# Attention and mixture of experts on one core: the value product's bank is emptied before the step's second row maximum, row maxima are transposed two steps behind, and the preparation of a pair is spread

## The chip, the cores and the metric

The kernel runs on one core of a Trainium2 chip. The metric is the device time of one execution in microseconds, here the median of three executions. An engine is named as the profile names it: PE (TensorE, matrix products; PEld is its loading of weights), DVE (VectorE), ACT (ScalarE), POOL (GpSimd) and SP, whose queue issues the transfers.

## What is computed

An attention over 8 batches of 8 heads, with queries averaged in twos, and a mixture of experts in which each token takes one of 8 experts:

```
q_pool = q.reshape(B, H, S // 2, 2, D).mean(axis=3)
scores = scale * q_pool @ k^T;  scores -= max(scores)
attn   = exp(scores);  attn /= sum(attn) + 1e-09
x      = attn @ v                      # 4608 tokens of 512
e_idx  = argmax(x @ w_gate)            # one expert for a token
out    = gate_w * sigmoid(x @ w_output_gate)[e_idx] * relu(x @ w1[e]) @ w2[e]
```

B and H are 8, S is 1152 (576 pooled queries), D is 64; an expert's inner width is 1024. Operands are split into a rounded part and a remainder (names ending in h and l), so most products are made of two or three matmuls.

## The kernel before

The 64 heads are taken two at a time: 32 pairs. A pair's work is cut into 18 **steps**, nine for each of its two heads (`body` calls `attention`, then `Moe.run`). A step holds, in the order in which the code records it for PE:

- the scores of 128 keys against 576 queries (L279 and L281, four matmuls into `sps`, a pool of two buffers of two banks each). ACT takes two exponentials of them (L293 and L294, or L285 and L286). In steps 1, 3, 7, 9, 13 and 15 of a pair (table `PLP`) the second exponential goes back into the same banks and DVE subtracts there (L289); in the others POOL subtracts in SBUF (L295) and the banks are free after L294;
- one or two tiles of **row maxima** for the pair after it (L232, two or three matmuls into `mp`, a ring of three banks, and a DVE reduction, L233). Even steps have one, odd steps have two;
- where nine or fifteen tiles are together, the transposing of their maxima (`rows`, L259, in the same ring of three banks), DVE's split of them into two rows (L262, L263) and two small transfers into row 66 and 67 of `qb`, from where the scores of the pair subtract them (L281);
- in even steps a burst of P V (L308 to L310, 15 matmuls for each 128 keys), six steps behind the scores. It sums into one bank, `av`, the only buffer of its pool. The first head's burst begins in step 6 of a pair and the second's in step 16. Ahead of each the bank must have been read by DVE: L317 and L320 make the factor `r`, L323 multiplies and is the last reader;
- pieces of the router's work (`logits`, `router`), in odd steps, which take banks of the same ring (L370, L385, L410).

DVE's small work goes through a list, `fill`. One entry is taken at a step's start and one after each reduction of maxima. The three entries of the bank's emptying (`e0`, `e1`, `e2`) are put at the head of that list when a head's last burst is recorded.

The **preparation** of a pair (loading, rounding on ACT, remainders on POOL, copies through SP's queue) stands in the table `PREP`: a number in thirds of a step, and a name. From pair 5 on (pairs are counted from 0) a third r lies (r - 9) / 3 steps behind the start of the preparation, which is 32 steps ahead of the pair; a pair is 54 thirds long, so r and r + 54 are the same place in consecutive pairs. On ACT are `kh` (two), `qh`, `amax` (two, each with a read of its sum) and `vh` (two).

PE, DVE, ACT and POOL run in the order of the code. SP's queue is ordered by the program's scheduler, which also decides which buffer of a pool a new tile gets; so a change of order can change the banks.

Of the kernel before, what the change touches and what calls it, by code (L numbers as in the profile page):

```python
# [20 lines left out]
L0 = 15.5  # L21
LS = 0.037
RI = 7
PREP = ((0, 'lk'), (12, 'kh', 0), (13, 'kh', 1), (12, 'qsum'), (15, 'kl'), (18, 'dk', 0), (19, 'dk', 1), (21, 'qh'), (26, 'ql'), (26, 'dq', 0), (27, 'dq', 1), (29, 'qd'), (32, 'dl', 0), (33, 'dl', 1),
        (53, 'lv'), (71, 'amax', 0), (74, 'amax', 1), (81, 'gmax'), (82, 'scale', 0), (85, 'scale', 1), (90, 'scale', 2), (93, 'vh', 0), (93, 'vs', 0), (96, 'vh', 1), (97, 'vl', 0), (100, 'vs', 1), (104, 'vl', 1))
BURST = {0: 2, 2: 2, 4: 2, 6: 2, 8: 1, 10: 2, 12: 2, 14: 2, 16: 3}
PLP = (1, 3, 7, 9, 13, 15)
PLPL = (1, 3, 5, 7, 9, 11, 13, 15, 17)
# [3 lines left out]
SKIP = 3  # L32
TS = 256
M_PAD = 1000
TLAG = 1
ALAG = 6
PB = 9
P32 = 6
# [21 lines left out]
def attention(tc, qT, kT, vL, wg, keep, xrows, idscr, cum, pairs, setup, scat, init):  # L60
    nc = tc.nc
    nb = len(pairs) // 4
    with ExitStack() as ctx:
# [36 lines left out]
        def dmaf(o, i):  # L100
            nc.sync.dma_start(out=o.bitcast(F32), in_=i.bitcast(F32))
# [143 lines left out]
        fill = []  # L245
        now = [0]

        def pop(k=1):
            while k and fill:
                fill.pop(0)()  # L250
                k -= 1
# [3 lines left out]
        def rows(force=False):  # L255
            while pend_t and (force or now[0] >= pend_t[0][-1] + TLAG):
                m9, nt, t0, t1, qbf, _ = pend_t.pop(0)
                tp = ps_m.tile([128, 512], F32, name="tp", tag="mp")[0:nt, 0:128]
                nc.tensor.transpose(out=tp, in_=m9[:, 0:nt], identity=ident)  # L259
                mr = sm.tile([5, 2, 128], F32R, name="mr")[0:nt]  # L260
                c0 = 16.0 * SHIFT
                nc.vector.tensor_scalar(out=mr[:, 0], in0=tp, scalar1=c0, scalar2=None, op0=ALU.subtract)  # L262
                nc.vector.scalar_tensor_tensor(out=mr[:, 1], in0=tp, scalar=c0, in1=mr.bitcast(F32)[:, 0], op0=ALU.subtract, op1=ALU.subtract)  # L263
                for j in range(2):
                    dmaf(qbf[66 + j:67 + j, 128 * t0:128 * t1].rearrange("o (t n) -> o t n", n=128), mr[:, j])
# [32 lines left out]
        def av(st, h, xb):  # L298
            vt = st['vt']
            a = ps_a.tile([128, 512], F32, name=f"av{st['n']}", tag="av")  # L300
            av_ = a[:, 0:325].rearrange("p (b x) -> p b x", x=65)
            pop(99)
            for c in range(NC):
                ph, pl = st['ph', h, c], st['pl', h, c]
                for qb in range(5):
                    q0 = 128 * qb if qb < 4 else NQ - 128
                    hi, lo = ph[:, q0:q0 + 128], pl[:, q0:q0 + 128]
                    nc.tensor.matmul(av_[:, qb, 0:65], lhsT=hi, rhs=vt[:, h, c, 0:65], start=c == 0 and qb == 0, stop=False)  # L308
                    nc.tensor.matmul(av_[:, qb, 0:64], lhsT=hi, rhs=vt[:, h, c, 66:130], start=False, stop=False)  # L309
                    nc.tensor.matmul(av_[:, qb, 0:65], lhsT=lo, rhs=vt[:, h, c, 0:65], start=False, stop=c == NC - 1 and qb == 4)  # L310
                if c < NC - 1:
                    yield
            r = sm.tile([128, 5], F32, name="r")
            H = 2 * st['p'][1] + h

            def e0():
                nc.vector.tensor_scalar(out=r, in0=av_[:, :, 64], scalar1=1e-9 * math.exp(SHIFT), scalar2=st['sc'][:, h:h + 1], op0=ALU.add, op1=ALU.mult)  # L317

            def e1():
                nc.vector.reciprocal(out=r, in_=r)  # L320

            def e2():
                nc.vector.tensor_tensor(out=xb[:, :, 64 * H:64 * H + 64], in0=av_[:, :, 0:64], in1=r.unsqueeze(2).broadcast_to([128, 5, 64]), op=ALU.mult)  # L323
                if h == 1:
                    routers.append([logits(st['p'][0], st['p'][1], xb), 0])
            fill[0:0] = [e0, e1, e2]
            pop(IMM)
            yield

# [31 lines left out]
        def logits(b, c, xb):  # L361

            xh = sm.tile([128, NQ], F32R, name="xh", bufs=1)
            xl = sm.tile([128, NQ], F32R, name="xl", bufs=1)
            yield 1
            for c0, c1, grp in ((0, 256, (0, 1)), (256, NQ, (2, 3, 4))):
                tx = psum()
                for i, t in enumerate(grp):
                    x = xb[:, t, 128 * c:128 * c + 128]
                    nc.tensor.transpose(out=tx[:, 128 * i:128 * i + 128], in_=x, identity=ident)  # L370
                d = 0
                for o, w in ((0, c1 - c0),) if c0 == 0 else ((0, 256), (320, 64)):
                    z = slice(c0 + d, c0 + d + w)
                    nc.scalar.copy(out=xh[:, z], in_=tx[:, o:o + w])

                    def sub(o=o, w=w, z=z, tx=tx):
                        nc.vector.tensor_tensor(out=xl[:, z], in0=tx[:, o:o + w], in1=xh.bitcast(F32)[:, z], op=ALU.subtract)
                    fill.insert(0, sub)
                    d += w
                yield 1  # L380
            for c0, c1 in ((0, 256), (256, NQ)):
                pop(99)
                tl = psum()
                for j, x in enumerate((xh, xl)):
                    nc.tensor.matmul(tl[:, 0:c1 - c0], lhsT=wgt[:, c], rhs=x[:, c0:c1], start=j == 0, stop=j == 1)  # L385
                if c == 0:
                    nc.vector.tensor_copy(out=lT[:, c0:c1], in_=tl[0:32, 0:c1 - c0])
                else:
                    nc.vector.tensor_tensor(out=lT[:, c0:c1], in0=tl[0:32, 0:c1 - c0], in1=lT[:, c0:c1], op=ALU.add)
                yield 1  # L390
            if c == 3:
                yield from router(b, xb)
# [111 lines left out]
        NP = len(pairs)  # L504
        pos = dict(m=0)

        def adv(k, g, want):
            while pos[k] < want:
                next(g, None)
                pos[k] += 1  # L510
# [3 lines left out]
        def prep_at(s, ph):  # L514
            u = 3 * (s + SLEAD) + ph
            for n in range(max(u // 54 - 2, 0), min(u // 54 + 2, NP)):
                r = u - 54 * n + min(3 * (LEAD - 15), 2 * n)
                if r == 0:
                    preps[n] = prep(n, PREP)
                if n in preps:  # L520
                    for f in preps[n].pop(r, ()):
                        f()

        E = mybir.EngineType
        with tc.manual_schedule(engines={E.PE, E.DVE, E.Activation, E.Pool}):
            for s in range(-SLEAD, 0):
                for ph in range(3):
                    prep_at(s, ph)
                if s == -RI:
                    for i in (1, 2):  # L530
                        dmaf(QBs[i][64:66], QBs[0][64:66])
                        dmaf(KBs[i][64:68], KBs[0][64:68])
                if s == 1 - SLEAD + INIT:
                    consts()
                    init(0)
                if s >= -int(L0):
                    adv('m', mg, int(1.5 * (s + 1 + L0)))
                    now[0] = s
                    pop(3)
                    rows()  # L540
            for s in range(18 * NP + 14):
                now[0] = s
                live = s < 18 * NP
                if s % 18 == 2 and 0 < s // 18 < 5:
                    init(s // 18)
                while pendv:
                    pendv.pop(0)()
                pop()
                if live:
                    next(sg)  # L550
                prep_at(s, 0)
                mw = min(27 * NP, int(1.5 * (s + 1 + min(LEAD, L0 + LS * s))))
                if pos['m'] < mw:
                    adv('m', mg, pos['m'] + 1)
                prep_at(s, 1)
                adv('m', mg, mw)
                rows()
                j = s - ALAG
                for _ in range(BURST.get(j % 18, 0) if 0 <= j < 18 * NP else 0):
                    next(ag)  # L560
                prep_at(s, 2)
                if not live:
                    pop(3)
                for r in routers:
                    if s % 2 or not live or not r[1]:
                        r[1] = next(r[0], 0)
            pop(99)
            for r in routers:
                for _ in r[0]: pass
# [420 lines left out]
```

## Time and profile before

| | |
|---|---|
| median of three executions | 1624.14 us (1623.79 to 1625.01) |
| the profiled execution | 1624.72 us |
| its span in the trace | 1622.7 us |
| mean granted clock of PE | 0.986 |
| attention, first scores to last | 34 to 1076 us |
| instructions | 42199 |

The time of the profiled execution is its span and some 2 us around it. In the trace a busy PE is not PE at its peak, and the end of a matmul is modelled; so what a wait costs is read from the starts of matmuls. Rows of the timeline give start and duration in us, then engine, line, operation, written tile and read tiles, and in brackets the idle time of the engine before it with what ended it.

### The profile page before, as it was taken

To read this page: it belongs to the slowest core of one execution; us is meant where nothing else is said; L and a number is where in the kernel's file an instruction comes from. 1 tells how busy PE (TensorE), PEld (TensorE's weight loads), DVE (VectorE), ACT (ScalarE), POOL (GpSimd) and SP (SyncE) were. 2 spreads that over 40 slices of the span, in tenths; PEclk is the share of its full clock that TensorE was granted. 3 is DMA by queue.
4 is the path that set the end of the run, shared out by engine and by line. 5 is a ranking of instruction groups with operands and counts; after the bars stand their busy time and mean duration, and the time that the engine had idled before them with its cause. 6 is when DMAs were issued, how large, how long until landed. Compare 5 with 4: busy or idle time off the path is not lost. (4 is left out here: it accounts for less than half of the span.)

```text
span 1622.7 us, 42199 instructions
## 1 busy us (share of the span) xinstructions
PE 1533.1 (94%) x16618; PEld 1411.1 (87%) x16618; DVE 1073.4 (66%) x2222; ACT 1078.5 (66%) x1862; POOL 996.3 (61%) x917
## 2 busy tenths in 40 slices
PE   4999999999999999999999999879999999999997
PEld 4898889888988888888888888868999999999996
DVE  4676776776676676676677767656666566656663
ACT  2887778877878787878777877744445444544541
POOL 4887888788879788879788978634222322232300
PEclk9999999999999999999999999979999999999999
DMA  7765455655566457446645664255454655263600
GB/s 207 217 160 143 133 149 149 156 139 141 152 151 158 124 144 189 129 123 175 158 129 153 161 154 127 83 173 196 168 190 156 213 176 194 94 226 107 208 22 25
DMA packets 88754, 245.48 MB, mean 151 GB/s; under 512 B 13082, under 2 KB 17370, under 8 KB 88546
## 3 DMA queue, kind: packets, MB, share of 16 engines
q1 hardware_dynamic: 78826, 221.07, 48.6%
q0 software_dynamic: 9728, 21.67, 4.2%
q8 instruction: 134, 2.20, 0.6%
q14 instruction: 66, 0.54, 0.1%
HBM read 165.04 MB, written 23.81 MB: 116 GB/s over the span
## 5 line engine op out<-in xcount | busy, mean ns | idle before, releaser
L233 DVE TENSOR_REDUCE pm<-mp 128x1 f32<-128x384 f32 x864 | 457.6, 549 | 263.3 <-PE mp L232 257.7
L295 POOL TENSOR_TENSOR pl<-p,ph 128x576 f16<-128x576 f32 x381 | 490.2, 1287 | 187.8 <-ACT ph L294 155.5
L232 PE MATMUL mp<-ka,qa 128*128 128x384 f32 x960 | 317.7, 347 | 20.2 <-DMA qa<-yq 18.5
L293 ACT ACTIVATE p<-sps 128x576 f32<-128x576 f32 x381 | 251.0, 659 | 116.8 <-PE sps L281 108.3
L308 PEld LDWEIGHTS <-ph 128*128 128x128 f16 x2880 | 262.6, 97 | 74.3 <-DVE xb L323 40.8
L308 PE MATMUL av<-vt,ph 128*128 128x65 f16 x2880 | 297.0, 194 | 23.4 <-DVE xb L323 23.4
L279 PE MATMUL sps<-qa,ka 128*128 128x288 f32 x1152 | 281.6, 326 | 16.7 <-ACT ph L294 10.9
L309 PE MATMUL av<-vt,ph 128*128 128x64 f16 x2880 | 294.7, 195 | 0.0
L310 PE MATMUL av<-vt,pl 128*128 128x65 f16 x2880 | 293.8, 193 | 0.0
L309 PEld LDWEIGHTS <-ph 128*128 128x128 f16 x2880 | 266.2, 97 | 0.4
L310 PEld LDWEIGHTS <-pl 128*128 128x128 f16 x2880 | 266.5, 99 | 0.0
L232 PE MATMUL mp<-kb,qb 66*128 66x384 f32 x768 | 262.5, 342 | 0.6 <-DMA kb<-kp 0.6
L281 PE MATMUL sps<-qb,kb 68*128 68x288 f32 x1152 | 248.5, 298 | 2.8 <-DMA qb<-mr 2.8
L294 ACT ACTIVATE ph<-sps 128x576 f16<-128x576 f32 x381 | 249.3, 654 | 0.0
L279 PEld LDWEIGHTS sps<-qa,ka 128*128 128x128 f32 x1152 | 183.5, 191 | 27.9 <-ACT ph L294 19.2
L764 PE MATMUL hps<-xh,w1h 128*128 128x256 f32 x704 | 200.4, 285 | 0.0
L764 PE MATMUL hps<-xl,w1h 128*128 128x256 f32 x704 | 200.3, 284 | 0.0
L232 PEld LDWEIGHTS mp<-ka,qa 128*128 128x128 f32 x960 | 180.4, 192 | 22.8 <-issue 18.5
L764 PE MATMUL hps<-xh,w1l 128*128 128x256 f32 x704 | 199.6, 284 | 0.0
L767 ACT ACTIVATE hh<-hps 128x512 fp32r<-128x512 f32 x88 | 52.7, 598 | 221.1 <-PE hps L764 221.1
L285 ACT ACTIVATE ph<-sps 128x576 f16<-128x576 f32 x195 | 128.9, 661 | 92.0 <-PE sps L281 89.7
L281 PEld LDWEIGHTS sps<-qb,kb 68*128 68x128 f32 x1152 | 186.7, 191 | 3.2 <-DMA qb<-mr 3.2
(170 smaller groups left out, 3184.6 us busy)
## 6 DMA issues: line engine op xcount, KB each, us to landing
ka<-xk SPq DMA_DIRECT2D x128, 288.0 KB
raw1b<-in_w_dram SPq DMA_DIRECT2D x24, 1024.0 KB
raw2b<-in_w_dram SPq DMA_DIRECT2D x24, 1024.0 KB
raw1a<-in_w_dram SPq DMA_DIRECT2D x22, 1024.0 KB
raw2a<-in_w_dram SPq DMA_DIRECT2D x22, 1024.0 KB
qp<-in_qT_dram SPq DMA_DIRECT2D x32, 576.0 KB
kpf<-in_kT_dram SPq DMA_DIRECT2D x32, 576.0 KB
vp<-in_vL_dram SPq DMA_DIRECT2D x32, 576.0 KB
```

What stands on the lines that cost most here:

```text
L232: nc.tensor.matmul(mp, lhsT=l, rhs=r, start=j == 0, stop=j == len(ops) - 1)
L233: nc.vector.tensor_reduce(out=pm[:, i:i + 1], in_=mp, axis=AX.X, op=ALU.max)
L279: nc.tensor.matmul(sps[:, j, 0:288], lhsT=ka[:, h, ks], rhs=qa[:, o + 288 * j:o + 288 * j + 288], start=True, stop=False)
L281: nc.tensor.matmul(sps[:, j, 0:288], lhsT=kb[:, h, ks], rhs=qb[:, h, 288 * j:288 * j + 288], start=False, stop=True)
L285: nc.scalar.activation(out=ph2, in_=x, func=AF.Exp, scale=1.0 / 16)
L293: nc.scalar.activation(out=p32.rearrange("p (j n) -> p j n", j=2), in_=x, func=AF.Exp, scale=1.0 / 16)
L294: nc.scalar.activation(out=ph2, in_=x, func=AF.Exp, scale=1.0 / 16)
L295: nc.gpsimd.tensor_tensor(out=pl, in0=p32, in1=ph, op=ALU.subtract)
L308: nc.tensor.matmul(av_[:, qb, 0:65], lhsT=hi, rhs=vt[:, h, c, 0:65], start=c == 0 and qb == 0, stop=False)
L309: nc.tensor.matmul(av_[:, qb, 0:64], lhsT=hi, rhs=vt[:, h, c, 66:130], start=False, stop=False)
L310: nc.tensor.matmul(av_[:, qb, 0:65], lhsT=lo, rhs=vt[:, h, c, 0:65], start=False, stop=c == NC - 1 and qb == 4)
L764: nc.tensor.matmul(hp[:, f], lhsT=W1[w][:, c, fs], rhs=d[x][:, c], start=i == 0, stop=i == 11)
```

## The change

It has four parts: the table `PREP` with other distances, `TLAG` 2 in place of 1, two of the three entries of the bank's emptying put into one, and, once the last maxima have been taken, two more entries of the list in each step.

```diff
-PREP = ((0, 'lk'), (12, 'kh', 0), (13, 'kh', 1), (12, 'qsum'), (15, 'kl'), (18, 'dk', 0), (19, 'dk', 1), (21, 'qh'), (26, 'ql'), (26, 'dq', 0), (27, 'dq', 1), (29, 'qd'), (32, 'dl', 0), (33, 'dl', 1),
-        (53, 'lv'), (71, 'amax', 0), (74, 'amax', 1), (81, 'gmax'), (82, 'scale', 0), (85, 'scale', 1), (90, 'scale', 2), (93, 'vh', 0), (93, 'vs', 0), (96, 'vh', 1), (97, 'vl', 0), (100, 'vs', 1), (104, 'vl', 1))
+PREP = ((0, 'lk'), (12, 'kh', 0), (12, 'qsum'), (19, 'kh', 1), (20, 'kl'), (21, 'dk', 0), (22, 'dk', 1), (26, 'qh'), (29, 'ql'), (28, 'dq', 0), (29, 'dq', 1), (32, 'qd'), (33, 'dl', 0), (35, 'dl', 1),
+        (63, 'lv'), (87, 'amax', 0), (93, 'amax', 1), (96, 'gmax'), (98, 'scale', 0), (99, 'scale', 1), (105, 'scale', 2), (106, 'vh', 0), (107, 'vs', 0), (109, 'vl', 0), (112, 'vh', 1), (112, 'vs', 1), (115, 'vl', 1))
...
-TLAG = 1
+TLAG = 2
...
-            def e0():
+            def e01():
                 nc.vector.tensor_scalar(out=r, in0=av_[:, :, 64], scalar1=1e-9 * math.exp(SHIFT), scalar2=st['sc'][:, h:h + 1], op0=ALU.add, op1=ALU.mult)
-
-            def e1():
                 nc.vector.reciprocal(out=r, in_=r)
...
-            fill[0:0] = [e0, e1, e2]
+            fill[0:0] = [e01, e2]
...
                 rows()
+                if pos['m'] == 27 * NP:
+                    pop(2)
```

On DVE, in steps 4 to 6 of pair 11, where the bank of pair 10's second head is emptied (`pm<-mp` are reductions of maxima: the first here is step 4's, the next two are step 5's, the last is step 6's, behind which PE starts the next sum). Before:

```order
L289 TENSOR_TENSOR pl<-sps_7936,ph 128x576
L233 TENSOR_REDUCE pm<-mp_7963 128x1
L317 TENSOR_SCALAR r<-av_7751,sc 128x5
L233 TENSOR_REDUCE pm<-mp_8027 128x1
L320 RECIPROCAL r<-r 128x5
L233 TENSOR_REDUCE pm<-mp_8033 128x1
L323 TENSOR_TENSOR xb<-av_7751,r 128x5x64
L233 TENSOR_REDUCE pm<-mp_8052 128x1
```

And now, at the same place (L318 and L321 are the old L320 and L323):

```order
L289 TENSOR_TENSOR pl<-sps_7934,ph 128x576
L233 TENSOR_REDUCE pm<-mp_7963 128x1
L317 TENSOR_SCALAR r<-av_7745,sc 128x5
L318 RECIPROCAL r<-r 128x5
L233 TENSOR_REDUCE pm<-mp_8028 128x1
L321 TENSOR_TENSOR xb<-av_7745,r 128x5x64
L233 TENSOR_REDUCE pm<-mp_8033 128x1
L233 TENSOR_REDUCE pm<-mp_8050 128x1
```

The bank's last reader has moved from behind both reductions of the step to between them.

On PE, in step 13 of pair 10, between two scores: two tiles of maxima and the router's logits (L385, now L383), which take a bank of the same ring. Before:

```order
L279 MATMUL sps_7658<-qa_125,ka_122 128x288 x2
L281 MATMUL sps_7658<-qb_128,kb_119 128x288 x2
L232 MATMUL mp_7666<-ka_120,qa_123 128x384
L232 MATMUL mp_7666<-kb_117,qb_126 128x384
L232 MATMUL mp_7670<-ka_120,qa_123 128x384
L232 MATMUL mp_7670<-kb_117,qb_126 128x384
L385 MATMUL tp<-xh,wgt 128x320
L385 MATMUL tp<-xl,wgt 128x320
```

And now:

```order
L279 MATMUL sps_7645<-qa_125,ka_122 128x288 x2
L281 MATMUL sps_7645<-qb_128,kb_119 128x288 x2
L232 MATMUL mp_7652<-ka_120,qa_123 128x384
L232 MATMUL mp_7652<-kb_117,qb_126 128x384
L232 MATMUL mp_7656<-ka_120,qa_123 128x384
L232 MATMUL mp_7656<-kb_117,qb_126 128x384
L259 MATMUL tp<-ident,m_7504 5x128
L383 MATMUL tp<-xh,wgt 128x320
L383 MATMUL tp<-xl,wgt 128x320
```

The transposing of the maxima, which stood in step 12 ahead of its burst of P V, has come between the maxima and the logits, so that four tiles of the ring of three banks follow each other. In the built program the logits' bank is the one of the step's first tile of maxima.

On PE, at the scores of step 17 of pair 10, behind the burst of step 16, with the engines whose semaphores an instruction waits for (Activation is ACT). Before:

```order
L310 LDWEIGHTS pl_7522
L310 MATMUL av10_7751<-vt0_138,pl_7522 128x65
L279 MATMUL sps10_7784<-qa1_125,ka1_122 128x288 [waits DVE_49,PE_49]
L279 MATMUL sps10_7784<-qa1_125,ka1_122 128x288
L281 MATMUL sps10_7784<-qb1_128,kb1_119 128x288 x2
```

And now:

```order
L310 LDWEIGHTS pl_7515
L310 MATMUL av10_7745<-vt0_138,pl_7515 128x65
L279 MATMUL sps10_7778<-qa1_125,ka1_122 128x288 [waits PE_49,Activation_49]
L279 MATMUL sps10_7778<-qa1_125,ka1_122 128x288
L281 MATMUL sps10_7778<-qb1_128,kb1_119 128x288 x2
```

Before, these scores took the buffer of step 15, free after DVE's subtraction; now they take the buffer of step 16, the step just ahead of them, free after its second exponential. Counted over the built program, scores follow scores in the same buffer in step 3 of 27 pairs before and 7 now, in step 15 of 28 pairs before and 28 now, and in step 17 of 8 pairs before and 31 now.

## The prediction

> **What bounds the kernel now.** I read the stretches first, then who waits for whom, then single steps in the timeline. Columns of a stretch are its length, busy time of PE, PEld, DVE, ACT and POOL, granted clock, share of DMA and GB/s.
>
> ```profile
> 200.00:1000.00 800.00, 769.02 (x10213) 710.77 (x10212) 564.39 (x1422) 639.20 (x1196) 657.49 (x586) 1.00 0.58 148
> 1043.00:1077.00 34.00, 25.33 (x381) 23.55 (x380) 15.61 (x28) 25.69 (x45) 15.07 (x15) 0.85 0.34 125
> 1052.80:1059.50 6.70, 4.35 (x44) 4.19 (x45) 6.04 (x8) 6.06 (x10) 1.29 (x1) 0.50 0.91 343
> 1118.00:1600.00 482.00, 482.00 (x3154) 441.84 (x3153) 305.95 (x328) 227.65 (x287) 124.32 (x115) 1.00 0.48 163
> ```
>
> PE sets the pace: 769 of 800 us in the even part of the attention, 482 of 482 in the experts, which the change doesn't touch. So only PE's waits in the attention can go. The next view gives them (us, times, longest); the first two rows are of the whole run, the others of 200 to 1000 us.
>
> ```profile
> PEld L308 <- DVE xb L323: 40.8, 56, 3.8
> PE av L308 <- DVE xb L323: 23.4, 53, 3.5
> ...
> PE av L308 <- DVE xb L323: 14.7, 43, 0.4
> PE sps L279 <- ACT ph L294: 9.4, 21, 0.5
> ```
>
> Two waits matter: P V for its bank, and scores for theirs. Here are steps 14 to 17 of pair 18 on PE, DVE and ACT.
>
> ```profile
> 646.34 0.33 PE L232 MATMUL mp<-kb,qb 66*128 66x384 f32 x1
> 646.51 0.20 PE L308 MATMUL av<-vt,ph 128*128 128x65 f16 x1
> 647.61 0.53 PE L279 MATMUL sps<-qa,ka 128*128 128x288 f32 x2 [0.46 <-ACT ph L294]
> 648.41 0.34 PE L232 MATMUL mp<-kb,qb 66*128 66x384 f32 x1
> 648.94 0.43 PE L279 MATMUL sps<-qa,ka 128*128 128x288 f32 x2
> 649.64 0.33 PE L232 MATMUL mp<-kb,qb 66*128 66x384 f32 x1
> 650.33 0.20 PE L308 MATMUL av<-vt,ph 128*128 128x65 f16 x1 [0.35 <-DVE xb L323]
> 651.25 0.51 PE L279 MATMUL sps<-qa,ka 128*128 128x288 f32 x2
> ```
> ```profile
> 648.78 0.56 DVE L233 TENSOR_REDUCE pm<-mp 128x1 f32<-128x384 f32 x1 [0.93 <-PE mp L232]
> 649.26 0.18 DVE L320 RECIPROCAL r<-r 128x5 f32<-128x5 f32 x1
> 649.35 0.52 DVE L233 TENSOR_REDUCE pm<-mp 128x1 f32<-128x384 f32 x1
> 649.79 0.48 DVE L323 TENSOR_TENSOR xb<-av,r 128x320 f32<-128x320 f32 x1
> ```
> ```profile
> 646.91 0.65 ACT L294 ACTIVATE ph<-sps 128x576 f16<-128x576 f32 x1
> ...
> 648.49 0.65 ACT L285 ACTIVATE ph<-sps 128x576 f16<-128x576 f32 x1 [0.27 <-PE sps L281]
> 649.04 0.65 ACT L286 ACTIVATE sps<-sps 128x576 f32<-128x576 f32 x1
> 649.61 0.76 ACT L187 ACTIVATE vt<-vp,sc 128x576 f16<-128x576 f32 x1
> ```
>
> Without a wait P V follows the last matmul of maxima by 0.17 (646.34 to 646.51). Here it comes at 650.33 in place of 649.81: the wait costs 0.52, not the 0.35 in the bracket. The scores of step 15 start 0.05 after the end of the second exponential of step 14 (646.91 + 0.65): they lie in step 14's own buffer. ACT had no backlog, and the preparation (L187) stands behind the exponentials, so this wait is one for a bank and not for a crowded ACT.
>
> [...]
>
> **The change part by part.** *A, the emptying.* L323 now stands behind the first reduction of its step (648.78, after which DVE takes the next instruction at 649.26) and no longer waits for the second tile. It starts at 649.26, and P V can follow 0.54 later, as now (649.79 to 650.33): at 649.80, against 649.81 without a wait. All 0.52 goes, with no margin. Of the 53 waits three lie behind 1050 us; of the other 50 I count in the timeline 29 in step 6 and 21 in step 16. Step 6: 29 x 0.52 = **-15.1**.
>
> In step 16 most of it comes back. The scores of step 17 now use step 16's buffer. Its exponentials start 0.88 after its scores (647.61 to 648.49), so at 649.82 (ACT is free by 649.61); the second follows 0.55 later and lasts 0.65: scores can start at 651.07, while P V would be done at 649.81 + 0.92 = 650.73. Gain 651.25 - 651.07 = 0.18, 21 x 0.18 = **-3.8**; bounds 0 and 0.52 each.
>
> *B, step 3.* The built program has 7 pairs with the same buffer in steps 2 and 3, in place of 27:
>
> ```profile
> 656.68 0.21 PE L308 MATMUL av<-vt,ph 128*128 128x65 f16 x1
> ...
> 657.82 0.53 PE L279 MATMUL sps<-qa,ka 128*128 128x288 f32 x2
> ```
>
> P V's 0.92 would end at 657.60, so 0.22 goes, 20 times: **-4.4**. Step 15's wait stays in 28 pairs; no spacing of ACT's work touches it, and I cost the spacing itself at nothing: ACT is busy 639 of 800 us and its preparation lies beside PE's work now too.
>
> *C, TLAG.* Before pairs with a router PE now and then waits for a bank of the ring of three:
>
> ```profile
> 330.01 0.34 PE L232 MATMUL mp<-kb,qb 66*128 66x384 f32 x1
> ...
> 331.00 0.27 PE L259 MATMUL tp<-ident,m 128*4 128x128 f32 x1 [0.31 <-DVE pm L233]
> ```
>
> So a tile that takes the bank of a tile of maxima starts no earlier than 0.99 after the last matmul of the latter. In the built program this happens anew in step 13 of 27 pairs: two tiles of maxima, the moved transposing, and the logits in the first tile's bank. Today that step and a transposing are:
>
> ```profile
> 644.81 0.34 PE L232 MATMUL mp<-kb,qb 66*128 66x384 f32 x1
> ...
> 645.34 0.31 PE L385 MATMUL tp<-xh,wgt 128*128 128x320 f32 x1
> ...
> 610.93 0.27 PE L259 MATMUL tp<-ident,m 128*5 128x128 f32 x1
> 611.04 0.19 PE L308 MATMUL av<-vt,ph 128*128 128x65 f16 x1
> ```
>
> With 0.11 for the transposing the logits are due at 645.45 and can start at 644.81 + 0.99 = 645.80: 0.35 lost, 27 x 0.35 = **+9.5**, bounds 0 and 0.46 each (12.4). The wait in the rows above goes in 7 pairs, but a like one comes in step 15 of 7 others, where the router's transposes take the first tile's bank: 0.
>
> *D, the sum of V's maxima* (L175 on PE) stood seven thirds behind ACT's second `amax` and is now three behind it, in step 15.
>
> ```profile
> L171 ACT ACTIVATE junk<-vp 128x576 f16<-128x576 f32 x64 | 44.6, 697 | 0.0
> ...
> L171 ACT ACTIVATION_READ_ACCUMULATOR junk<-vp 128x1 f32 x64 | 13.8, 216 | 0.0
> ```
>
> `amax` can start some 0.57 after 646.91 and ends 0.91 later at most, 648.39; with 0.05 PE has it at 648.44, and would want it 0.62 after 647.61, at 648.23. Up to 0.21; as both engines overlap their instructions I take 0.1, in 31 pairs **+3**, bounds 0 and 6.5.
>
> *E, the end of the attention.*
>
> ```profile
> 1055.15 0.23 PE L308 MATMUL av<-vt,ph 128*128 128x65 f16 x1 [3.53 <-DVE xb L323]
> ...
> 1073.09 0.20 PE L308 MATMUL av<-vt,ph 128*128 128x65 f16 x1 [2.29 <-DVE xb L323]
> ...
> L733 ACT CAST w1h<-raw1a 128x1024 fp32r<-128x1024 f32 x44 | 42.9, 1046 | 1.0 <-DMA raw1a<-in_w_dram 1.0
> ```
>
> With the list emptied at once both waits go, 5.8 us. But ACT is as busy as PE there (25.7 and 25.3 of 34 us), and the four casts of weights that hid in the first wait now stand one by one between exponentials: 4 x 1.05 = 4.2 at most. I take two thirds of it back, **-3**, bounds 0 and -5.8. The clock is at half behind the 3.53 us wait (6.7 us in the third row of the first view).
>
> [...]
>
> *F, the start.*
>
> ```profile
> PE sps L281 <- DMA qb<-mr: 2.8, 2, 2.2
> ```
>
> The first two pairs' scores already wait for their maxima. These are now transposed a step later and queue behind two to four copies on SP: I take **+3**, bounds 0 and 6.
>
> Sum: -15.1 - 3.8 - 4.4 + 9.5 + 3 - 3 + 3 = -10.8. On the profiled execution's own 1624.72 that is 1613.9; it lay 0.6 above the median, so **1613**.
>
> **Rivals.** *All that is emptied early is kept, and the ring doesn't stall:* 50 x 0.52 and 5.8, 31.8 us, 1592. For it: DVE may take the step's first reduction sooner than I think; against: the buffers of step 17 and the bank of step 13 are fixed by the program. 0.10.
>
> *The emptying comes too late all the same.* My margin is 0.01 us. If L323 ends 0.25 late in most places, some 8 us of A are lost: 1621. 0.12.
>
> *Spacing does shorten ACT's waits in step 15:* 28 x 0.5 more, 1599. Against it: the 0.05 above. 0.05.
>
> *Maxima land too late, and it gets slower.* The transfer of a pair's first maxima to `qb`:
>
> ```profile
> 645.80 1.58 SPq L101 DMA_DIRECT2D qb<-mr  x2
> ...
> 652.84 0.42 PE L281 MATMUL sps<-qb,kb 68*128 68x288 f32 x2
> ```
>
> It is issued by 647.38 and read at 652.84: 5.5 us. `kh`, `qh`, `ql` and the copies ahead of it on SP move two to seven thirds back and the transposing three; a step is 1.8 us, so 1.8 to 3.6 of the 5.5 go. From there each further microsecond of landing time is paid in 31 pairs: 0.5 us late gives 1629, 1 us 1644. It decides where landing takes over 2 to 4 us. 0.05. The lengthened preparation of V is covered: its last POOL work ends in step 3 of the pair, P V reads it from step 6 on.
>
> **How the numbers follow.** The forecast has 0.68, its own range is 1606 to 1619. A measurement of this kernel can tell about 0.2% from no change, so faster means below 1620.9. Faster: 0.68 + 0.10 + 0.05 and a quarter of the late emptying, 0.86; same 0.09; slower 0.05. The 8-in-10 range leaves out the first rival and the last and reaches to the two others: 1602 to 1620.
>
> **What would show it.** Right: P V's bank gone from PE's waits; step 16 to 17 at about 2.1 us with scores starting 0.05 behind L294; a wait of the logits (L383) for DVE in step 13 of most pairs; step 15 unchanged. Wrong: waits of P V for L321 that stay, scores waiting for `qb<-mr` in every pair, or step 13 as short as before (1.61 us).

## The result and the profile after

The changed kernel takes **1651.75 us** (median of 4, 1650.52 to 1653.37), against 1623.97 us for the kernel before on the same chip: a ratio of 1.0162, 95% interval 1.0148 to 1.0175. 1613 had been forecast, with a range of 1602 to 1620; it is the last rival that came about, and it cost more than its 1629 to 1644. The profiled execution has a span of 1651.7 us and a mean granted clock of 0.978, before 0.986. What is read from a profile below is one execution: that of the changed kernel took 1653.37 us, the highest of its four, and those of vprep and after_qs3 took 1629.09 and 1636.65 against medians of 1621.85 and 1630.11.

The same views as before the change. Stretches first (length, busy time of PE, PEld, DVE, ACT and POOL, granted clock, DMA share, GB/s); the second is a stretch at half clock (0.50), which begins while PE waits, from 402.2 to 405.4 us.

```profile
200.00:1000.00 800.00, 760.28 (x9870) 701.63 (x9870) 547.51 (x1366) 622.06 (x1151) 634.59 (x566) 0.98 0.56 142
403.70:410.50 6.80, 5.07 (x42) 4.80 (x43) 0.71 (x2) 2.64 (x5) 3.02 (x4) 0.50 0.16 48
```

PE does 9870 matmuls in the 800 us in which it did 10213, and the clock, which was 1.00 there, is 0.98. Who waits for whom in these 800 us (us, times, longest):

```profile
PEld sps L281 <- DMA qb<-mr: 20.1, 10, 3.4
PE sps L281 <- DMA qb<-mr: 17.0, 9, 3.2
...
PEld tp L383 <- DVE pm L233: 12.5, 23, 0.5
PE sps L279 <- ACT ph L294: 10.5, 23, 0.5
...
PEld L308 <- DVE xb L321: 6.7, 42, 0.2
```

P V's weight loads wait 0.2 for the bank at most, its matmuls no longer at all. The wait of the logits (L383) has come as forecast, and step 15's wait (L279) has stayed. New is the first: scores that wait for the maxima in `qb`, in the middle of the kernel; over the whole run PE waits for them in 12 pairs of 32, before in two.

The end of the attention has moved from 1080.2 to 1109.5 us, 29.3 later; the part behind it takes 542.5 and 542.2 us. Cut at the start of each step's scores, the 29.3 are made up of

| | us |
|---|---|
| first scores of a pair waiting for the maxima (27.6 in all, 3.1 before) | +24.5 |
| all else in steps that lie at half clock in one of the two kernels (29 after, 11 before) | +11.7 |
| all else in steps at full clock in both | -6.5 |
| start of the first scores | -0.5 |

The third row is the part that the forecast had been about: its terms A to D came to -10.8, and E and F cancelled. Its steps, over the pairs at full clock: 6: -13.8; 16: -6.3; 10: -5.0; 1: -4.4; 12: -2.6; 2 and 3: -2.9; 13: +15.6; 15: +11.0. The second row has gains in it too: -6.4 in pair 31 and -3.6 in pair 3; against these stand 21.7 in nine pairs.

### The profile page after: what moved, and what is told of

It is laid out like the page before. It is cut to its first block, busy times and chain, and to the rows that moved or that the text cites. A ratio compares the mean times of both kernels' runs of the same rounds, so it can differ in the third digit from the quotient of the medians.

```text
span 1651.7 us, 42269 instructions
## 1 busy us (share of the span) xinstructions
PE 1548.7 (94%) x16618; PEld 1423.7 (86%) x16618; DVE 1078.2 (65%) x2222; ACT 1084.3 (66%) x1862; POOL 994.5 (60%) x917
## 5 line engine op out<-in xcount | busy, mean ns | idle before, releaser
L232 PE MATMUL mp<-ka,qa 128*128 128x384 f32 x960 | 322.4, 352 | 20.7 <-DMA qa<-yq 18.5
L279 PE MATMUL sps<-qa,ka 128*128 128x288 f32 x1152 | 283.5, 328 | 21.1 <-ACT ph L294 13.8
L281 PE MATMUL sps<-qb,kb 68*128 68x288 f32 x1152 | 252.7, 302 | 25.4 <-DMA qb<-mr 24.3
L232 PE MATMUL mp<-kb,qb 66*128 66x384 f32 x768 | 266.3, 347 | 0.6 <-DMA kb<-kp 0.6
L294 ACT ACTIVATE ph<-sps 128x576 f16<-128x576 f32 x381 | 247.3, 649 | 0.0
L281 PEld LDWEIGHTS sps<-qb,kb 68*128 68x128 f32 x1152 | 190.2, 194 | 28.3 <-DMA qb<-mr 28.0
L279 PEld LDWEIGHTS sps<-qa,ka 128*128 128x128 f32 x1152 | 188.3, 194 | 29.9 <-ACT ph L294 17.3
L285 ACT ACTIVATE ph<-sps 128x576 f16<-128x576 f32 x195 | 126.8, 650 | 55.1 <-PE sps L281 51.8
```

What stands on the lines that cost most here:

```text
L232: nc.tensor.matmul(mp, lhsT=l, rhs=r, start=j == 0, stop=j == len(ops) - 1)
L279: nc.tensor.matmul(sps[:, j, 0:288], lhsT=ka[:, h, ks], rhs=qa[:, o + 288 * j:o + 288 * j + 288], start=True, stop=False)
L281: nc.tensor.matmul(sps[:, j, 0:288], lhsT=kb[:, h, ks], rhs=qb[:, h, 288 * j:288 * j + 288], start=False, stop=True)
L285: nc.scalar.activation(out=ph2, in_=x, func=AF.Exp, scale=1.0 / 16)
L294: nc.scalar.activation(out=ph2, in_=x, func=AF.Exp, scale=1.0 / 16)
```

## Where the maxima were held up

The first scores of pair 19 on PE:

```profile
674.95 0.42 PE L279 MATMUL sps<-qa,ka 128*128 128x288 f32 x2
677.71 0.50 PE L281 MATMUL sps<-qb,kb 68*128 68x288 f32 x2 [2.33 <-DMA qb<-mr]
```

L281 follows L279 by 0.27 without a wait; here by 2.76, so 2.5 us are lost. What SP issued ahead of it (start, duration; a row with x4 holds four transfers):

```profile
660.34 0.33 SPq L125 DMA_DIRECT2D qp<-in_qT_dram  x1
660.77 4.14 SPq L101 DMA_DIRECT2D ka<-xk  x4
...
671.20 0.86 SPq L101 DMA_DIRECT2D kb<-kp  x1
672.16 1.58 SPq L101 DMA_DIRECT2D qb<-mr  x2
```

DVE had split the maxima by 668.46, yet they are issued at 672.16 to 673.74: twelve copies stand ahead of them. These are K and Q of pair 20, whose own scores are 48 us away; to pair 19 they matter only because its maxima stand behind them. They start at 660.77, 14.2 us ahead of pair 19's scores (from here on, "ahead of a pair" is meant so). Pair 20's K had been cast by 657.65. What the copies stand behind is the load of the *next* pair's queries, those of pair 21 (L125), which may go only when POOL has read the buffer (L139, `qsum`). POOL, and the same two places in the kernel before:

```profile
653.91 1.23 POOL L194 TENSOR_TENSOR vt<-vp,vt 128x576 f16<-128x576 f32 x1
...
656.55 1.06 POOL L475 DMA_INDIRECT idscr<-tid,posi  x1 [0.17 <-issue]
...
658.88 1.43 POOL L139 TENSOR_TENSOR yq<-qp 128x576 f32<-128x576 f32 x1
```
```profile
632.83 1.44 POOL L139 TENSOR_TENSOR yq<-qp 128x576 f32<-128x576 f32 x1
```
```profile
634.30 0.33 SPq L125 DMA_DIRECT2D qp<-in_qT_dram  x1
634.73 4.04 SPq L101 DMA_DIRECT2D ka<-xk  x4
```

In both kernels the load goes 0.03 us after `qsum` ends (660.31 and 634.27) and K's copies 0.43 behind it. Before, that is 17.8 us ahead of pair 19's scores (652.57), and 17.8 to 17.9 in pairs 7, 11, 15 and 20; after, 13.4 to 14.2 us in pairs 7, 11, 15 and 19 and 17.3 in pair 20. In the late pairs POOL also has the router's writes (L475), and V's last remainder (L194), which used to be 16 thirds of a step away, now stands 5 thirds ahead of `qsum`. `qsum` itself kept its place in the table.

A late start of the copies covers pairs 7, 11, 15 and 19, which lose 9.8 of the 20.1 us that go from pair 2 on. Another 9.8 go in pairs 6, 10, 14, 18, 22 and 26, where K's copies start 17.5 to 17.8 us ahead, only 0.6 to 1.0 later than before. In these pairs the router writes a batch's rows (`xrows`, 1026 KB). Pair 18 in the changed kernel, then before:

```profile
622.87 0.33 SPq L125 DMA_DIRECT2D qp<-in_qT_dram  x1
623.29 0.39 SPq L459 DMA_DIRECT2D xrows<-xb  x1
623.80 6.28 SPq L101 DMA_DIRECT2D ka<-xk  x4
...
638.02 1.57 SPq L101 DMA_DIRECT2D qb<-mr  x2
```
```profile
602.03 3.76 SPq L101 DMA_DIRECT2D ka<-xk  x4
...
613.75 1.57 SPq L101 DMA_DIRECT2D qb<-mr  x2
615.38 0.43 SPq L461 DMA_DIRECT2D xrows<-xb  x1
```

The write now stands between the load and the copies; before, it stood behind the maxima. K's four copies take 6.28 us to issue in place of 3.76, and the maxima go out 14.2 us behind the first of them in place of 11.7. DVE had finished the rows at 621.23, but the write, too, stood behind the load, which POOL let go at 622.84. So it is the same chain in a second form.

That this chain is the cause was a reading of rows so far; the runs test it.

## The experiments

All times are medians; the kernel before, run along, took 1622.8 to 1623.9 us. Line numbers in experiments made from the changed kernel are its own.

### Which part of the change

**merge_tail**: the changed kernel without the new table and without `TLAG`.

```diff
-TLAG = 2
+TLAG = 1
```
(and `PREP` of the kernel before)

> The changed kernel with the old PREP and TLAG 1, so of the change only the two edits to the emptying of the bank are left. Theory: these two are a gain, and the loss comes from the late maxima (qb<-mr) and from the ring. Then steps 6 lose 0.5 us each (29 x 0.5 = 14), steps 16 keep nearly all of theirs, because here the scores of step 17 share the buffer of step 16 in 11 pairs and not in 31 (some 8), the last pair ends 4 earlier: 1624 - 26 = 1598 us, no waits of scores for qb<-mr beyond the first two pairs. Rival (the edits of the emptying are worth nothing by themselves, or the waits come back elsewhere): 1615 to 1624.

1610.73 us, ratio 0.9927 (0.9910 to 0.9944). No waits for maxima, as expected, and step 6 is 0.50 shorter; but step 8 is 0.39 longer, which gives back 7.7 us. ACT and DVE in steps 7 and 8 of pair 10, and PE's scores of step 9:

```profile
369.98 1.25 ACT L133 CAST xk<-kpf 128x576 fp32r<-128x576 f32 x2
...
371.66 0.66 ACT L294 ACTIVATE ph<-sps 128x576 f16<-128x576 f32 x1
372.19 0.70 ACT L171 ACTIVATE junk<-vp 128x576 f16<-128x576 f32 x1
...
372.85 0.67 ACT L285 ACTIVATE ph<-sps 128x576 f16<-128x576 f32 x1
373.38 0.68 ACT L286 ACTIVATE sps<-sps 128x576 f32<-128x576 f32 x1
```
```profile
374.16 0.76 DVE L289 TENSOR_TENSOR pl<-sps,ph 128x576 f16<-128x576 f32 x1 [0.82 <-POOL pl L295]
```
```profile
375.07 0.37 PE L279 MATMUL sps<-qa,ka 128*128 128x288 f32 x1 [0.22 <-DVE pl L289]
```

The scores of step 9 need step 7's buffer, which DVE's subtraction (L289) holds until 374.92. The subtraction is late because step 7's exponentials are: two casts of K (L133) and an `amax` (L171) stand on ACT ahead of L285. (The bracket at L289 names POOL, whose subtraction happened to end at 374.16; L286 ends at 374.06, and in kprep, too, L289 starts 0.11 behind it.) While P V waited for its bank in step 6, ACT had 0.5 us to catch up.

**lag1**: the changed kernel with `TLAG = 1`.

> The changed kernel with TLAG 1, so with the new PREP. Theory: the late maxima need both edits, one takes 1.9 us of lead, the other makes SP issue its copies later. With TLAG 1 the maxima go out some 2 us earlier, ahead of the last two copies: waits for qb<-mr fall from 27.6 us to under 6 and the half clock behind them goes, the logits no longer wait in step 13 (12 us less), against it 4 us in step 3 and 3 in step 1: 1605 to 1615 us. Rival (the copies of the new PREP alone make them late): the waits stay near 25 us, 1635 to 1645.

1643.89 us, 1.0132 (1.0110 to 1.0155), where the rival had put it. K's copies start 13.2 us ahead of pairs 11, 15 and 19; the maxima are split 2 us earlier, and then wait up to 5.0 us for SP. Waits for `qb<-mr` are halved (13.8 us), but in step 1 of pairs 6, 10, 14 and 22 the transposing (L259) waits 1.2 to 1.7 us for DVE, which itself has stood 3.4 to 3.9 us for POOL's part of V's scale (L184 for L182), and 22 steps are at half clock.

**oldprep**: the changed kernel with the old `PREP`.

> The changed kernel with the old PREP, so with TLAG 2. Theory (both edits are needed for the late maxima): the maxima are made 1.9 us later than before, yet wait less on SP; waits for qb<-mr stay under 6 us in all, the logits' wait in step 13 stays (12 us): 1598 + 12 - 5 = 1605 us, 1600 to 1612. Rival (TLAG alone makes them late): 20 us or more of waits for qb<-mr and some half clock, 1630 to 1640.

1625.13 us, 1.0009 (0.9997 to 1.0020). `TLAG` alone makes no maxima late: SP issues them as soon as they are split, 5.2 us before they are needed. But against merge_tail it costs 14.4 us: step 13 is 0.56 longer (19.6 us over all pairs; the transposing itself, 0.1, comes from step 12) and the first two pairs take 6.5 more, while steps 1, 2 and 12 give back some 12.

**mr_actq**: the changed kernel, the two transfers into `qb` from ACT's queue.

```diff
-                    dmaf(qbf[66 + j:67 + j, ...], mr[:, j])
+                    nc.scalar.dma_start(out=qbf[66 + j:67 + j, ...], in_=mr[:, j].bitcast(F32))
```

> The changed kernel with the two small transfers into qb issued from ACT's queue and not from SP's, so not behind the copies. Theory (they are late because they stand behind the copies on SP): waits for qb<-mr fall from 27.6 us to under 5, with the half clock behind them; 1651.7 - 24 - 10 = 1618 us, less up to 17 more because the built program has the same buffer in steps 14 and 15 of only 1 pair. Against it ACT waits for DVE's split of the maxima at each issue, of unknown price, up to 0.5 us x 64 = 32. Rival (they land late because the data of the copies is still moving when they are issued): the waits stay at 15 us or more although the issue is earlier.

1711.90 us, 1.0562 (1.0537 to 1.0586). The waits for `qb<-mr` went (1.7 us in all), so the maxima were late for standing behind the copies. But the price on ACT was far above the 32 us allowed for (pair 18):

```profile
654.09 1.62 ACTq L265 DMA_DIRECT2D qb<-mr  x2
655.75 0.65 ACT L293 ACTIVATE p<-sps 128x576 f32<-128x576 f32 x1 [1.76 <-DVE pl L289]
```

The two issues hold ACT for 1.62 us, until 655.71, and the exponentials behind them start that much later (the bracket names DVE's subtraction, but that had ended at 655.42); 68 steps are at half clock.

### Which line of the table

**kprep** and **vprep**: merge_tail with one line of the new `PREP` each, K's and Q's or V's.

> Only the first line of the new PREP (K and Q: kh, kl, dk, qh, ql, dq, qd, dl) beside the two edits of the emptying. Theory POOL: the copies start little later, no waits for them to speak of, 1605 to 1613 us. Rival (K's and Q's line): waits for qb<-mr or kb<-kp of 10 us or more and half clock, 1625 to 1645.

> Only the second line of the new PREP (V: lv, amax, gmax, scale, vh, vs, vl) beside the two edits of the emptying; K's and Q's line and TLAG are the old ones. Theory POOL: V's four operations on POOL (thirds 107 to 115, that is up to 7 of the next pair) now stand just ahead of the next pair's qsum (third 12); POOL runs behind, the load that waits for qsum stands on SP ahead of the copies of K, and so every copy and the maxima go out late. Then this line alone makes it slow: 10 us or more of waits for copies (qb<-mr, kb<-kp) and half clock, 1625 to 1640 us. Rival (K's and Q's line does it, by its later kh, kl and copies): no such waits, and 4 us more than the 1610.7 of merge_tail for the moved sum of the maxima, less up to 8 for a less crowded ACT in step 7: 1605 to 1615.

kprep 1644.36 us, 1.0115 (1.0076 to 1.0154); vprep 1621.85, 0.9985 (0.9968 to 1.0002). Neither theory holds as it was put: each line does harm by itself. vprep shows POOL's delay (`qsum` ends 15.4 us ahead of pairs 7, 11, 15 and 19, before 18.3) and waits for maxima in pairs 7, 11, 15, 19 and 23; the router's write stands behind the maxima there. kprep has few such waits, 2.7 us in all behind the start, and in other pairs: 6, 10, 14 and 26, where the write stands directly ahead of K's copies. So each line brings one of the chain's two forms. kprep's larger loss is 3 to 5 us at a time ahead of the scores of step 8 in pairs 6, 10, 14, 18 and 22 (ACT, SP and POOL around step 7 of pair 18):

```profile
650.56 0.67 ACT L133 CAST xk<-kpf 128x576 fp32r<-128x576 f32 x1 [5.36 <-DMA kpf<-in_kT_dram]
```
```profile
643.87 0.35 SPq L129 DMA_DIRECT2D vp<-in_vL_dram  x1
644.27 1.32 SPq L126 DMA_DIRECT2D kpf<-in_kT_dram  x1
```
```profile
642.61 1.24 POOL L194 TENSOR_TENSOR vt<-vp,vt 128x576 f16<-128x576 f32 x1
```

It is the same chain with other members: V's load waits for POOL's remainder of V (642.61 + 1.24 = 643.85, and the load goes at 643.87), K's load stands behind it on SP, and ACT, whose order is fixed, stands 5.36 us at the cast of K with the exponentials behind it.

### Letting SP go

**after_qact**: the changed kernel with the queries' load on ACT's queue, where nothing it must wait for is open any more.

```diff
-                nc.sync.dma_start(out=qp, in_=qT[b, hp]...)
+                nc.scalar.dma_start(out=qp, in_=qT[b, hp]...)
```

> The changed kernel with the load of the next pair's queries issued from ACT's queue, so that SP's queue no longer stops at it until POOL has made qsum of this pair. Theory (POOL is behind in the pairs with the router's writes; SP stops at this load, and all copies and the maxima behind it go out 3 to 4.5 us late): K's copies start some 17 us ahead of their pair in every pair and not 13.4 to 14.6, waits for qb<-mr fall from 27.6 us to under 8, half clock mostly goes: 1625 us (1612 to 1632); more is held back by ql, POOL's too. Rival (the maxima land late because they are transposed a step later, whatever stands ahead on SP): waits of 20 us or more stay, 1640 to 1652.

1631.16 us, 1.0042 (1.0025 to 1.0059): 20.6 us less than the changed kernel. SP and POOL for pair 19 of it, whose scores begin at 658.10:

```profile
640.83 3.50 SPq L101 DMA_DIRECT2D ka<-xk  x4
...
653.97 1.90 SPq L101 DMA_DIRECT2D qb<-mr  x2
```
```profile
642.01 1.42 POOL L139 TENSOR_TENSOR yq<-qp 128x576 f32<-128x576 f32 x1
```

K's copies no longer wait for `qsum`; they start 17.3 us ahead, before POOL has even begun it. POOL is as late as it was (`qsum` ends 14.7 us ahead, as in the changed kernel), and nobody waits for maxima any more but the first two pairs. The router's write is let go as well: it leaves as soon as the rows are ready, 2.5 us ahead of K's copies, and these take 3.4 to 3.5 us. The maxima were transposed as late as in the changed kernel, so that alone was not the cause.

**after_qs3**: the changed kernel with `(3, 'qsum')` in place of `(12, 'qsum')`.

> The changed kernel with qsum on POOL at third 3 in place of 12, so ahead of V's last two operations of the pair before; SP's queue is as in the changed kernel. Theory: as in after_qact, by the other end: the load is let go some 3 us earlier, K's copies start at 17 us ahead; waits for qb<-mr under 10 us, 1627 us (1612 to 1635). Rival: waits stay, 1640 to 1652; or the K and V remainders, now behind qsum, are late in its place.

1630.11 us, 1.0032 (1.0020 to 1.0045). The same chain let go at its other end gives the same time: `qsum` ends 19.9 us ahead of pairs 7, 11, 15 and 19, K's copies start at 16.9, and the write again has a lead of 2.5 us on the copies.

**lag1_qact**: lag1 with the load on ACT's queue.

> lag1 (whole new PREP, the emptying, TLAG 1) with the load of the next queries on ACT's queue. Theory: with SP not stopped, what is left of the new PREP is a gain at step 8 (8 us against merge_tail) and a cost of the moved sum of V's maxima (0.36 in step 15 less 0.23 in step 10, 4 us): 1610.7 - 8 + 4 + up to 8 of waits that stay = 1607 to 1616. Rival (the new PREP is slow for other reasons than SP's stop): 1630 to 1645.

1620.13 us, 0.9971 (0.9959 to 0.9982), 23.8 less than lag1 but above the range given, since pair 26 takes 40.75 us (its neighbours 32.6 and 32.2) and pairs 4, 16 and 20 have half clock behind step 15.

### What was left

**after_qact_fix**: after_qact with the two DVE operations that find the first full expert, once in the kernel, put into one that reads PSUM.

```diff
-        V.tensor_copy(out=cn, in_=cp[:, 0:8])
...
-        V.tensor_reduce(out=mx, in_=cn, axis=AX.X, op=ALU.max)
-        V.tensor_tensor(out=cn, in0=cn, in1=mx.broadcast_to([128, 8]), op=ALU.is_equal)
+        V.tensor_reduce(out=mx, in_=cp[:, 0:8], axis=AX.X, op=ALU.max)
+        V.scalar_tensor_tensor(out=cn, in0=cp[:, 0:8], scalar=mx, in1=em, op0=ALU.is_equal, op1=ALU.mult)
...
-        V.tensor_tensor(out=cn, in0=cn, in1=em, op=ALU.mult)
```

> after_qact with the two DVE operations at L648 and L650 (two operands in SBUF each) put into one that reads PSUM and SBUF. Theory: DVE's operation with two operands in SBUF waits until POOL pauses; that held up pair 26 by some 8 us (41.7 us, others 31.6 to 34). Then no DVE operation there takes over 1 us, pair 26 takes some 33.5 us and the time is 1631.2 - 8 = 1623 us (1620 to 1627). Rival (the stall comes from POOL or a transfer and L648 only shows it): 1629 to 1632.

1628.09 us, 1.0023 (1.0008 to 1.0038), 3 less than after_qact and not 8, and the two intervals overlap: the new operation takes 0.23, but the stall has moved to the next operation with two operands in SBUF (L652, 5.83 us, shown at the end), and pair 26 still takes 39 us.

**after_gmax**: the same with `amax` at 84 and 90 and `gmax` at 95.

> after_qact_fix with the two amax at 84 and 90 and gmax at 95 in place of 87, 93 and 96, so the sum of V's maxima stands behind step 14's burst and no longer in step 15. Theory: step 15 loses its 0.36 and step 14 gains 0.23, 31 x 0.13 = 4 us; the half clock behind step 15 of pairs 8, 12, 16, 20 came from that step's idle time, and goes, 5 us more: 1623 - 9 = 1614 us (1610 to 1619). Rival (half clock has nothing to do with the sum's place): 1618 to 1623 with as many stretches of half clock.

1616.37 us, 0.9957 (0.9946 to 0.9969). Step 15 is 0.35 shorter, as expected. Step 14 has not grown by the 0.23 expected: the sum now fills part of the time in which PE waited for step 14's exponentials, and that wait is 0.25 in place of 0.46 (`PE sps L279 <- ACT ph L294`: 6.1 us, 24 times; in the changed kernel 10.5, 23 times). One stretch of half clock stands behind a step 15 (pair 4); after_qact_fix had two (pairs 12 and 20), after_qact four. With SP let go, DVE's operation replaced and the sum moved, the changed kernel is thus near the 1613 forecast for it.

**mid83**: merge_tail with `amax` at 77 and 80 and `gmax` at 83 (and the first two pieces of `scale` at 84 and 86), POOL's operations on V left where they were.

> merge_tail with only the two amax moved apart from kh (77 and 80 in place of 71 and 74; gmax 83, scale 84 and 86 in place of 81, 82, 85); POOL's operations on V stay where they were. Theory: in merge_tail 0.39 us of each step 8 went to scores of step 9 that wait for step 7's subtraction (L289), which is late because ACT takes two casts and two amax in steps 6 to 8 and so reaches step 7's exponentials 1.2 us late. With amax later that wait goes, 20 x 0.39 = 8 us: 1603 us (1600 to 1607). Rival (DVE itself is late in step 8): the wait stays, 1608 to 1613.

1602.65 us, 0.9862 (0.9829 to 0.9896). Step 8 is back at 2.06 us: the crowding of ACT was the cause.

**mt_alt**, **mid83_alt**: the scores' buffers in strict turn.

```diff
-sps = ps_s.tile([128, 2, 512], F32, name=f"sps{st['n']}", tag="sps")
+sps = ps_s.tile([128, 2, 512], F32, name=f"sps{st['n']}", tag=f"sps{(c + h) % 2}", bufs=1)
```

> merge_tail with the scores' two buffers taken in strict turn (by the step's parity), so no step's scores follow in the buffer of the step just ahead. Theory: the waits of steps 15 (0.62 in 24 pairs, 15 us) and 3 (0.22 in 26 pairs, 6 us) and the rest of step 16 to 17 are waits for that buffer and go: 1610.7 - 20 = 1590 us (1586 to 1598). Rival (ACT or DVE is late there anyway, and the scores wait for the other buffer as long): 1606 to 1611.

> mid83 and the strict turn of the scores' buffers together. In mt_alt the turn gave 5.4 us, as step 15 then waited 0.42 for step 13's subtraction in place of 0.62 for step 14's exponentials. Theory: the two are independent, 1602.65 - 5.4 = 1597 us (1594 to 1600). Rival (step 9 or 15 waits for DVE's subtraction again): 1601 to 1606.

1605.33 us, 0.9882 (0.9850 to 0.9915), and 1603.99, 0.9884 (0.9867 to 0.9900). In place of the 0.62 for step 14's exponentials step 15 waits 0.42 for step 13's subtraction; 5.4 us are won on merge_tail, whose interval just touches this one, and nothing that can be told on mid83, where pair 26 and the start vary by as much.

**mid83_fix**, **mid83_alt_fix**: the last two with the DVE operation of after_qact_fix.

> mid83 with the same one DVE operation in place of L648 and L650. Theory: pair 26 takes 33 us in place of 37.6, 1602.65 - 4.4 = 1598 us (1596 to 1600). Rival: 1601 to 1604.

> mid83_alt with the same DVE operation. Theory: 1604 - 3 = 1601 us (1597 to 1603), not faster than mid83_fix beyond 0.2%, as the strict turn puts a wait for DVE's subtraction in place of that for ACT. Rival (the turn is worth 5 us): 1592 to 1596.

1599.94 us, 0.9861 (0.9845 to 0.9878), and **1597.91 us, 0.9839 (0.9822 to 0.9855)**, the fastest of all. Pair 26 takes 32.3 and 31.6 us. Both beat the kernel before, by 1.4 and 1.6%; between them the intervals overlap. The even part of the attention in mid83_alt_fix:

```profile
200.00:1000.00 800.00, 779.95 (x10440) 727.17 (x10437) 580.39 (x1447) 652.68 (x1219) 671.87 (x601) 1.00 0.60 151
```

## Why the prediction was wrong

*What bounds the kernel.* Right in that PE's waits in the attention were what could be won or lost. Wrong in "ACT had no backlog": it was read in steps 14 to 17. In steps 6 to 8 ACT is crowded, and the wait for P V's bank hid that (merge_tail, mid83).

*A, the emptying.* Right: step 6 lost 0.50 in nearly every pair (13.8 us in the pairs at full clock, 15.1 forecast). The count was off: the rows of the kernel before give 27 waits in step 6, 24 in step 16 and two behind 1050 us, not 29, 21 and three, which moves the sum by less than 1 us. Step 16 gave 6.3 and not 3.8, as its exponentials start 0.74 and not 0.88 behind its scores. That the early emptying pays in full only with the spaced preparation was not seen.

*B* gave 2.9 of 4.4.

*C, the ring.* Right in place and kind, in 27 pairs as forecast, but too small: 0.46 in each step 13 (0.56 less the transposing's 0.1), which is the upper bound given, and not 0.35; 13.0 us in steps 12 and 13 and not 9.5.

*D* and the exchange of waits between steps 1 and 15: +1.6 us for steps 1, 10 and 15 together, +3 forecast. The half clock that follows step 15 in some pairs was not in it.

*E.* The last pair's scores and bursts take 33.1 us in place of 37.3, a gain of 4.2 for the 3 forecast, and the half clock there has gone (1.00 from 1076 to 1110 us). In the kernel before, the clock had fallen before the first long wait was over: at 1052.83, 1.2 us into the wait that ends at 1055.15, with PE busy for 1.93 of the 3.41 us ahead of the fall.

*F* was +3 with bounds 0 and 6; the first two pairs took 8.4 us more. PE ran at half clock for 17 us there, from 35.0 us on, within a wait of 4.5 that ended at 38.3.

*The step that failed* is the lead of the maxima: the sum put their waits from pair 2 on at nothing, and the rival "Maxima land too late" got a chance of 0.05. These waits cost 20.1 us, and those of the first two pairs 7.4. By the prediction's own numbers 1.9 to 3.7 us were left for a landing that it put at 2 to 4, so 0.05 was too little even then. Its reserve of 5.5 us was right: 5.46 in the rows. "So 1.8 to 3.6 of the 5.5 go" was not: in pair 19 the issue ends at 673.74 and the data are wanted at 675.22, 1.5 us later, so 4.0 had gone, and landing then took 4.0 (677.71 - 673.74). (Over the changed kernel's waits, landing took 1.8 to 4.5.) The prediction had moved the copies by their thirds in the table, and not quite rightly: the casts and remainders move by 0 to 6 thirds, the copies by 1 to 3, not two to seven. SP does not go by the table: its order was left to the scheduler, which puts the next load ahead of the copies, and that load goes when POOL has done. So what mattered was POOL, busy 657 of 800 us, and looked at only for P V's sake. The view of SP's own waits in the kernel before (200 to 1000 us) would have said it:

```profile
SPq L129 <- POOL vt L194: 199.7, 25, 9.3
SPq L125 <- POOL yq L139: 190.1, 24, 8.9
```

Three quarters of what SP waits for there is POOL (390 of 522 us). after_qact and after_qs3 show the chain by undoing one link each, and mr_actq by going round it. Its second form, the write against the copies, is less firmly shown, as no run moves the write alone. But in the three kernels in which it goes directly ahead of K's copies and the maxima behind them (the changed one, lag1, kprep) K's copies take 5.6 to 6.5 us in the six pairs and in 16 of these 18 cases the scores lose 0.15 to 1.9 us; in before, merge_tail, vprep, oldprep, after_qact, after_qs3 and lag1_qact, where the write goes elsewhere, they take 3.4 to 4.5 and none of the six pairs waits. Also missing from that rival's price was the half clock that came with the waits; and the waits came in 12 pairs, not in all 31.

Still open is why `TLAG` costs the start so much, by what the write slows the issue of the copies, and how a stretch is chosen for half clock (below).

## What to carry to other kernels

A queue that waits in order is only as early as its first entry (SP's copies of K went 0.43 us behind the load ahead of them, in both kernels): before moving work on an engine that is busy four fifths of the time, list which loads wait for a buffer that this engine reads, and what stands behind them. A wait on the pacing engine can hide another engine's backlog (merge_tail: step 6 0.50 shorter, step 8 0.39 longer); when it is removed, look two or three steps on for who used that time. Price a lateness that comes in bursts of some 2 us with the clock it may lose, not only with its own length: in the changed kernel waits of 1.9 us (pairs 22 and 26) had half clock with them, and one of 2.5 (pair 19) had none.

## What the runs showed of the hardware

**DVE held up by POOL.** In pair 26 a comparison of 128 x 8 elements stands on DVE, once in the kernel. In the kernel before, then in the changed one with POOL's rows:

```profile
897.75 0.28 DVE L648 TENSOR_TENSOR cn<-cn,mx 128x8 f32<-128x8 f32 x1
```
```profile
927.92 4.26 DVE L648 TENSOR_TENSOR cn<-cn,mx 128x8 f32<-128x8 f32 x1
```
```profile
927.04 1.27 POOL L295 TENSOR_TENSOR pl<-p,ph 128x576 f16<-128x576 f32 x1
928.27 2.65 POOL L136 TENSOR_TENSOR kp<-kpf,xk 128x1152 fp32r<-128x1152 f32 x1
930.89 2.57 POOL L295 TENSOR_TENSOR pl<-p,ph 128x576 f16<-128x576 f32 x2
```

It ends at 932.18, with the first of POOL's last two subtractions (932.15); the operation that ran when it started (until 928.31), and the next (L136, until 930.92), had ended with the comparison still running. POOL was busy in the kernel before too (18.45 of the 20 us from 885 on, 19.25 of those from 915 on in the changed one), but there the operation beside it ended at 898.01, and the comparison at 898.03. In after_qact_fix, where it has no second operand in SBUF, the next that has two stalls instead:

```profile
909.47 5.83 DVE L652 TENSOR_TENSOR oh<-em,mx 128x8 f32<-128x8 f32 x1
```
```profile
914.01 1.26 POOL L295 TENSOR_TENSOR pl<-p,ph 128x576 f16<-128x576 f32 x1
915.23 0.52 POOL L150 CAST qd<-xq 64x64 fp32r<-64x64 f32 x2
```

It ends at 915.30, the subtraction at 915.27. Other operations of this place with two operands in SBUF do likewise: L654 of the kernel before takes 1.06 us and ends at 902.37, POOL's subtraction at 902.35; L661 of the changed kernel takes 1.03 and ends at 939.00, POOL's at 938.99. Where POOL stood idle (934.82 to 937.70 in the changed kernel) L654 takes 0.16, and L651, with one operand, takes 0.16 with POOL at work (933.52 to 933.68). Why L648 ended with the third operation of POOL's and not with the first was not shown. The lost time is inside the operation's duration (4.26 us) and not in idle time ahead of it, so no view of waits shows it.

**Half clock without a long wait.** Stretches of half clock begin and end on a grid of 3.41 us (in the changed kernel they last 3.41, 6.83, 10.24 or 17.07, all but the last, which the end of the trace cuts off, and 468.51 and 738.17 us are 79 of these apart). Those at 468.51, 738.17 and 871.29 us of the changed kernel follow no wait over 0.5 us; the 3.41 us ahead of each, step 15 of pairs 12, 20 and 24, have PE busy for 2.65 to 2.67. After one with 2.06 (from 673.31 on) the clock stayed full. Of the eight such stretches between 400 and 940 us none follows 3.41 us in which PE stood still: it was busy for 1.4 to 2.7 of them. With the sum of V's maxima out of step 15 (after_gmax) there was one such stretch in place of two to four, which is few to judge by; by what measure the clock decides was not found.
